# Strided attention and AFNO mixing: the first 64 rows of v by another queue, and a later start of the doubled stores

## The chip, the cores and the metric

The kernel runs on one core of a Trainium2 chip. The metric is device time in microseconds (us) of one execution, here the median of several executions. Lower is better. The profile's own clock starts with the core's first instruction; its span is the time from there to the last instruction.

## The reference

Batch 8, 8 heads, 576 tokens, head dimension 64; then a Fourier mixing layer over the 512 model columns, of which only the first 64 frequencies carry weights. All inputs and the output are fp32.

```
scores = scale * q @ k.T                       # (B, H, S, S)
mask: heads 0-3  0 <= i-j < 32                 # local
      heads 4-7  i >= j and i % 32 == j % 32   # strided
x  = softmax(where(mask, scores, -1e9)) @ v    # to (B, S, 512)
X  = rfft(x, axis=1);  Y = zeros
Y[:, :64] = einsum('bmd,mde->bme', X, w_r + i*w_i)
u  = x + irfft(Y)
out = u + relu(u @ w_ch)                       # fp32
```

The two weight tensors w_r and w_i have 64 x 512 x 512 fp32 values each, 134 MB together: most of what is read.

## The kernel before

All work is put in order by hand (`manual_schedule`): each engine runs its instructions in the order in which the program text emits them, and waits only for semaphores of the data that it needs.

**Loading.** Inputs are read as fp32 and written to SBUF as fp16, the conversion being done by the transfer. All such loads are issued by GpSimd (POOL), one after another: q, k, v of the strided heads (`load_str`, lines 222 to 226), of the local heads (`load_loc`, line 233), and the weights (`w_fetch`, lines 187 to 194). `load_str` puts v, q and k of a batch into slots of the tile `ring`. Each slot holds 72 rows (4 heads x 18 blocks of 32 tokens) of 2048 values. For the first two batches rows 0 to 63 come singly for each batch (line 224, 256 KB of fp16), rows 64 to 71 for both at once (line 226, 64 KB); later batches come in pairs (line 222, 512 KB). SyncE (SP) loads the constants cT (the Fourier table, rows of 1152 bytes) and cMl (a mask), ScalarE's queue (ACT) loads cI (the identity) and the masks cM6 and cM5 (line 109).

**Start.** The order in the text is: `load_str(0, 1)`, ACT's constants, `load_str(1, 1)`, SP's constants, `strided_tokens()` (two small fills and a rearranging copy of cT on POOL, lines 331 to 333), `load_str(2, 2)`, and the first weights. POOL therefore stands at the copy of cT before it issues the loads of batch 2. Meanwhile VectorE (DVE) clears a tile (line 820), TensorE (PE) turns the identity 14 times as filler (line 823), and then `str_front(0)` turns v, q and k of batch 0 on PE, with evacuations by DVE and ACT. `str_v(0, 0)` comes first; it needs all 72 rows of v (PE at line 280).

**Middle.** Strided attention for 8 batches, then local attention, interleaved with products of the spectra with the weights ("modes", lines 601 and 644). Weights live in a ring of buffers, and three early weight pairs lie as guests in tiles that are used later: pair 7 lies in the tile with the tag "YT" (8 KB per partition). POOL issues a weight load when PE has read the buffer's former content.

**Tail.** After the last weight, 18 items are computed in the order of `items`: for each, PE adds the last spectra to two accumulators, ACT (and POOL for one half) makes the ReLU part (`v_done`), and DVE adds the two halves and SP stores them (`u_done`, lines 1094 to 1122). An item is two times 128 rows x 512 columns of fp32, 256 KB each. Items 0 to 9 store each half as soon as it is added, in rows of 2 KB (line 1120). From item 10 to 15, `double(k)` holds: the two items of a pair (even and odd output rows of the same batches) are put side by side in SBUF and are stored together by the second one, as two stores of 512 KB whose rows are 4 KB (line 1109). Items 16 and 17 store both halves at once in rows of 2 KB (line 1122).

Of the kernel before, what the change touches and what calls it, by code (L numbers as in the profile page):

```python
# [10 lines left out]
FP = mybir.dt.float32  # L11
# [45 lines left out]
def kernel(  # L57
# [10 lines left out]
    nc = tc.nc  # L68
# [3 lines left out]
    big = ctx.enter_context(tc.tile_pool(name="big", bufs=1))  # L72
# [63 lines left out]
    ring = pat.tile([128, 12, 2048], F16, name="ring")  # L136
# [73 lines left out]
    def loc_in(b, vi):  # L210
        t = ring[:, ds(2 * (b % 6), 2), :].rearrange("p n x -> p (n x)")
        return t[:, ds(1152 * vi, 1152)]

    def load_str(b, nb):
        for vi in (2, 0, 1):
            n = 3 * (b % 4) + SLOT[vi]
            two = ring[:, n : n + 4 : 3, :]
            src = SRC[vi][b - b % 2 : b - b % 2 + 2, 4:8].rearrange(
                "b h (c r) d -> (h c) b (r d)", r=32
            )  # L220
            if nb == 2:
                nc.gpsimd.dma_start(two[0:64], src[0:64])
            else:
                nc.gpsimd.dma_start(ring[0:64, n, :], src[0:64, b % 2])
            if b % 2 == 0:
                nc.gpsimd.dma_start(two[64:72], src[64:72])
# [27 lines left out]
    def act_copy(out, in_):  # L254
        nc.scalar.activation(out=out, in_=in_, func=ACTF.Copy)  # L255
# [4 lines left out]
    def str_q(b, g):  # L260
        qn, qT = str_in(b, 0), qTs[b % 2]
        tp = psum("tp", half=True)
        for i in range(8):
            nc.tensor.transpose(
                tp[:, ds(72 * i, 72)],
                qn[:, ds(128 * (8 * g + i), 128)],
                idn[0:72, 0:72],
            )
        nc.vector.tensor_copy(
            out=qT.rearrange("p (h r c) -> p r h c", h=4, r=16)[:, ds(8 * g, 8)],  # L270
            in_=tp[:, 0:576].rearrange("p (r h c) -> p r h c", h=4, c=NCB),
        )
# [32 lines left out]
    def str_k(b, j):  # L305
        str_turn(b, 1, j)

    def str_v(b, j):
        str_turn(b, 2, j)

    def str_back(b, part):
        tp = psum("tp", half=True)
        tv = tp.rearrange("p (g x) -> p g x", x=128)
        vg = v16[b % 2]
        js = (1, 2) if part else (0,)
        for i, j in enumerate(js):
            a, z = JG[j]
            for h in range(4):
                nc.tensor.transpose(
                    tv[:, 4 * i + h, :],  # L320
                    vT[:, ds(72 * a + h * (z - a) * NCB, 128)],
                    idn,
                )
        n = 90 if part else 108
        (act_copy if part else nc.vector.tensor_copy)(
            out=vg[0:n, ds(4 * js[0], 4 * len(js)), 2:130],
            in_=tv[0:n, 0 : 4 * len(js), :],
        )
# [461 lines left out]

    psum_pools(tp=3, sc=3, av=2)
    load_str(0, 1)
    const_load(nc.scalar, "cI", "cM6", "cM5")
    load_str(1, 1)
    const_load(nc.sync, "cT", "cMl")
    strided_tokens()
    load_str(2, 2)
    w_fetch()

    def str_front(b):  # L800
        return [
            lambda: str_v(b, 0), lambda: str_v(b, 1),
            lambda: str_v(b, 2), lambda: str_q(b, 0),
            lambda: str_back(b, 0),
            lambda: str_back(b, 1), lambda: str_q(b, 1),
            lambda: str_k(b, 0),
            lambda: str_k(b, 1), lambda: str_k(b, 2),
        ]
# [12 lines left out]
    fill = psum("tp", half=True)  # L821
    for i in range(14):
        nc.tensor.transpose(fill[0:64, ds(64 * i, 64)], idn[0:64, 0:64], idn[0:64, 0:64])
    first = str_front(0)
    for i, w in enumerate(first):
        w()
# [43 lines left out]
    for b in range(B):  # L870
# [12 lines left out]
        n = 0  # L883
        nm = NMODES[b]
        for mi in range(nm):
# [3 lines left out]
            n = upto  # L889
# [120 lines left out]
    for n, i in enumerate([3, 5, 7] + list(range(8, 21))):  # L1010
        b, t = n // 2, n % 2 * 2
# [42 lines left out]
    def out_rows(b, t):  # L1054
        if t < 4:
            steps = [[2 * DM, 128], [(S + 64) * DM, 2], [1, DM]]
            first = 256 * (t // 2) + t % 2
        else:
            steps = [[DM, 128], [2 * S * DM, 2], [1, DM]]
            first = 512  # L1060
        return bass.AP(
            tensor=out.tensor, offset=out.offset + (S * b + first) * DM, ap=steps
        )

    def double(k):
        return 10 <= k < 16

    def both_rows(b, t):
        return bass.AP(
            tensor=out.tensor,  # L1070
            offset=out.offset + (S * b + 64 * (b % 2) + 256 * (t // 2)) * DM,
            ap=[[2 * DM, 128], [1, 2 * DM]],
        )
# [20 lines left out]
    def u_done(k):  # L1094
        bs, t = items[k]
        up, rl = ups.pop(k), rls.pop(k)
        if not osbs:
            osbs.append(pw.tile([128, 2 * NWBUF, 2, DM], FP, tag="w", bufs=1, name="osb"))
        a = k % (2 * NWBUF)
        if double(k):  # L1100
            two = osbs[0][:, a - t % 2 : a - t % 2 + 2].rearrange(
                "p s h d -> p (s h) d"
            )
            for j in range(2):
                nc.vector.tensor_tensor(
                    out=two[:, 2 * j + t % 2], in0=up[:, j], in1=rl[:, j], op=AluOp.add
                )
                if t % 2:
                    nc.sync.dma_start(
                        both_rows(bs[j], t),  # L1110
                        two[:, 2 * j : 2 * j + 2].rearrange("p h d -> p (h d)"),
                    )
            return
        osb = osbs[0][:, a]
        for j in halves:
            nc.vector.tensor_tensor(
                out=osb[:, j], in0=up[:, j], in1=rl[:, j], op=AluOp.add
            )
            if k < 10:
                nc.sync.dma_start(out_rows(bs[0], t)[:, j], osb[:, j])  # L1120
        if k >= 10:
            nc.sync.dma_start(out_rows(bs[0], t), osb)

    flush()
# [23 lines left out]
    for k in range(2):  # L1148
        if k:
            u_early(k)  # L1150
        new_rows(k, ups[k], yys)
        u_done(k)
    for k in range(2, LAST + 2):
        if k == 7:
            held = psum("p", pair=True)[:, 0]
            spec_z(3, 1, held)
            act_copy(zzs[1], held)
        early = 2 if k == 2 else k - 1 if k > 3 else 0
        if k <= LAST:
            v_early(k)  # L1160
        if k > 3:
            u_early(early)
        if k <= LAST:
            new_rows(k, vps[k], zzs)
        if k == 2:
            u_early(k)
        if early:
            new_rows(early, ups[early], yys)
        if k <= LAST:
            v_done(k)  # L1170
        if early:
            u_done(early)
# [31 lines left out]
```

## Time and profile before

| | us |
|---|---|
| device time, median of 3 (range) | 424.64 (424.12 to 424.69) |
| the profiled execution | 424.68 |
| its span | 422.9 |
| PE, DVE, ACT, POOL busy | 327.6, 236.0, 219.8, 111.9 |
| first load of v issued by POOL, L224 | 1.24 to 1.93 |
| first product of the last weight, PE L644 | 390.76 |
| first store issued, SP L1120 | 394.98 |
| last store issued, SP L1122 | 417.7 |

The profile's slices show the share of busy time of each engine and the bytes that the 16 DMA engines wrote per second. For a load that turns fp32 into fp16 the bytes counted are those written, half of those read. The DMA share can exceed 1, since packets of one engine overlap. A "landing" is the time from the issue of a transfer to its completion.

### The profile page before, as it was taken

How to read it: one execution, taken by the hardware profiler on the slowest of the kernel's cores; microseconds unless marked ns; L12 is line 12 of the kernel's file. 1: busy time of each engine (PE TensorE's matmuls, PEld its weight loads, DVE VectorE, ACT ScalarE, POOL GpSimd, SP SyncE). 2: the span in 40 equal slices, each digit the busy share in tenths (PEclk: the TensorE clock that was granted, in tenths of full speed). 3: DMA queues.
4: the chain of work that ended last, by engine and by line, in shares of the span. 5: the costliest groups of instructions: out<-in, count | busy, mean ns of one | idle time of the engine just before them, and what ended most of it. 6: DMA issues, size and time to landing. Idle time of an engine off the chain costs nothing.

```text
span 422.9 us, 9776 instructions
## 1 busy us (share of the span) xinstructions
PE 327.6 (77%) x4156; PEld 202.2 (48%) x4156; DVE 236.0 (56%) x485; ACT 219.8 (52%) x407; POOL 111.9 (26%) x183
## 2 busy tenths in 40 slices
PE   3977878679999298789775858586679839888993
PEld 3865767564666155556533425253335413445320
DVE  3888768950364234555315527656276455555895
ACT  1777768742666166576653413532163345444783
POOL 7432333322421011113121211211112212210583
PEclk9999979956999779899989969999689978999998
DMA  8999999999999999999999999999999999997598
GB/s 148 212 214 213 214 212 213 210 211 211 214 213 213 214 215 214 215 213 215 211 215 214 213 215 213 215 212 213 214 213 215 214 213 215 212 214 155 211 357 326
DMA packets 29674, 91.62 MB, mean 217 GB/s; under 512 B 3968, under 2 KB 4736, under 8 KB 29632
## 3 DMA queue, kind: packets, MB, share of 16 engines
q0 software_dynamic: 24624, 81.28, 96.8%
q1 hardware_dynamic: 4576, 9.65, 6.1%
q8 instruction: 32, 0.52, 0.5%
q10 hardware_dynamic: 432, 0.08, 0.1%
q14 instruction: 10, 0.08, 0.0%
HBM read 162.83 MB, written 9.44 MB: 407 GB/s over the span
## 4 chain that ended last, share of the span: by engine, by line
DMA 56%; PE 27%; DVE 8%; issue 4%; ACT 3%; POOL 1%; DVEq 0%; POOLq 0%; ACTq 0%
DMA wring<-in_moe_w_i_dram 42%; DMA ring<-in_q_dram 7%; PE y L601 7%; DMA wring<-in_moe_w_r_dram 4%; PE sc L743 3%; PE p L1030 2%; DMA ring<-in_k_dram 2%; PE p L1050 2%; PE tp L417 2%; PE sc L463 1%; PE sc L536 1%; DVE xb L245 1%; DVE yy L778 1%; DMA ring<-in_v_dram 1%; PE sc L479 1%
## 5 line engine op out<-in xcount | busy, mean ns | idle before, releaser
L601 PE MATMUL y<-wring,X 128*32 128x512 f16 (+1 forms) x424 | 47.9, 443 | 34.8 <-DMA wring<-in_moe_w_i_dram 34.7
L190 POOL DMA_DIRECT2D wring<-in_moe_w_r_dram x39 | 23.6, 604 | 188.3 <-PE y L601 163.2
L255 ACT ACTIVATE yr<-y 128x512 f16<-128x512 f32 x28 | 16.7, 597 | 57.3 <-PE y L601 55.6
L601 PEld LDWEIGHTS <-X 128*32 128x32 f16 (+1 forms) x448 | 21.9, 143 | 47.9 <-DMA wring<-in_moe_w_i_dram 34.4
L753 DVE COPY xo<-tp 128x512 f16<-128x512 f16 x32 | 22.1, 692 | 36.2 <-PE tp L751 36.2
L743 PE MATMUL sc<-w_cp,xT 128*128 128x512 f16 x128 | 37.1, 413 | 1.5 <-DVE xT L711 1.4
L245 DVE TENSOR_TENSOR xb<-av,rec 90x256 f16<-90x256 f32 (+2 forms) x80 | 36.0, 450 | 2.8
L752 ACT ACTIVATE v<-sc 128x512 f16<-128x512 f32 x32 | 19.1, 597 | 35.4 <-PE sc L743 35.4
L493 ACT ACTIVATE PL<-sc 128x480 f16<-128x480 f32 (+1 forms) x48 | 26.9, 578 | 17.2 <-PE sc L479 16.7
L244 DVE RECIPROCAL rec<-av 90x4 f32<-90x4 f32 (+2 forms) x80 | 14.6, 183 | 34.7 <-PE av L508 24.3
L424 DVE COPY qT<-tp 128x576 f16<-128x576 f16 x16 | 11.9, 752 | 36.7 <-PE tp L417 36.7
L1004 DVE TENSOR_TENSOR xo<-p,xo 128x1024 f16<-128x1024 f32 x16 | 19.6, 1225 | 20.3 <-PE p L786 20.3
L190 POOL DMA_DIRECT2D wring<-in_moe_w_i_dram x42 | 25.4, 606 | 9.7 <-DMA wring<-in_moe_w_i_dram 5.8
L382 ACT ACTIVATE PL<-sc 90x360 f16<-90x360 f32 (+1 forms) x48 | 22.7, 490 | 6.6 <-PE sc L375 6.2
L255 ACT ACTIVATE v<-p 128x1024 f16<-128x1024 f32 x16 | 16.4, 1023 | 18.3 <-PE p L786 18.3
L417 PE MATMUL tp<-cI_s,ring 64*64 64x64 f16 x864 | 23.5, 201 | 2.3 <-DVE qT L424 1.7
L255 ACT ACTIVATE v<-tp 128x640 f16<-128x640 f16 (+1 forms) x24 | 19.0, 807 | 10.5 <-PE tp L451 7.9
L463 PE MATMUL sc<-cMl_s,cI_s 128*128 128x480 f16 (+1 forms) x48 | 19.3, 401 | 4.7 <-ACT PL L493 3.1
L417 PEld LDWEIGHTS <-ring 64*64 64x64 f16 x864 | 18.7, 115 | 8.5 <-issue 4.4
L255 ACT ACTIVATE kz<-tp 64x360 f16<-64x360 f16 (+1 forms) x32 | 18.9, 592 | 6.2 <-PE tp L417 5.2
L1090 POOL TENSOR_TENSOR rl<-rl,xo 128x512 f32<-128x512 f32 x15 | 17.1, 1157 | 15.5 <-DVE rl L1083 13.0
L536 PEld LDWEIGHTS <-xb 108*128 108x128 f16 (+2 forms) x176 | 15.7, 107 | 11.2 <-DVE xb L245 6.2
(153 smaller groups left out, 763.6 us busy)
## 6 DMA issues: line engine op xcount, KB each, us to landing
wring<-in_moe_w_r_dram POOLq DMA_DIRECT2D x17, 1024.0 KB, 18.1
wring<-in_moe_w_i_dram POOLq DMA_DIRECT2D x16, 1024.0 KB, 22.4
wring<-in_moe_w_i_dram POOLq DMA_DIRECT2D x24, 512.0 KB, 17.6
wring<-in_moe_w_r_dram POOLq DMA_DIRECT2D x22, 512.0 KB, 15.2
out_dram<-osb SPq DMA_DIRECT2D x20, 256.0 KB, 2.3
out_dram<-osb SPq DMA_DIRECT2D x8, 512.0 KB, 3.5
ring<-in_v_dram POOLq DMA_DIRECT2D x8, 288.0 KB, 13.2
ring<-in_q_dram POOLq DMA_DIRECT2D x8, 288.0 KB, 13.5
```

The source lines that it names most:

```text
L190: nc.gpsimd.dma_start(dst, rows)
L245: nc.vector.tensor_tensor(out=dst, in0=val.rearrange("p h (q c) -> p h c q", c=4), in1=rec[0:n, 0:pieces] .to_broadcast((n, pieces, 64)) . ...
L255: nc.scalar.activation(out=out, in_=in_, func=ACTF.Copy)
L382: nc.scalar.activation(out=PS[0:n, ds(POFF[t], 4 * n)], in_=scp[0:n, 0 : 4 * n], func=ACTF.Exp, scale=SCALE,)
L417: nc.tensor.transpose(tp[ds(64 * hp, 64), ds(64 * i, 64)], qn[ds(64 * hp, 64), ds(64 * (9 * g + i), 64)], idn[ds(64 * hp, 64), ds(64 * hp, ...
L463: nc.tensor.matmul(scp[:, 0 : n * times].rearrange("p (h x) -> p h x", h=times), idn, mask_rows("cMl", n, times), start=True, stop=False,)
L493: nc.scalar.activation(out=dst, in_=src, func=ACTF.Exp, scale=SCALE)
L536: nc.tensor.matmul(xp[:, ds(192 * cp, 192)].rearrange("p (f m) -> p f m", f=3), xb[b][0:n, base + t, ds(128 * cp, 128)], F[0:n, :, t, :], ...
L601: nc.tensor.matmul(yp[ds(a, 32), :], Xh[half][pr, c].rearrange("p b r (h m) -> p (b r h) m", h=2)[:, :, mm % 32], wt[pr, XC[c], :], start= ...
L743: nc.tensor.matmul(vp, xT[:, ch], w_chs["cp"][:, ch, :], start=(ch == 0), stop=(ch == 3),)
L753: nc.vector.tensor_copy(out=xo.rearrange("p (h q c) -> p h q c", h=2, c=4), in_=tp[:, 0:512].rearrange("p (h c q) -> p h q c", h=2, c=4),)
L1004: nc.vector.tensor_tensor(out=xo, in0=up[:, 0:n], in1=xo, op=AluOp.add)
```

## The change

In `load_str`, the load of rows 0 to 63 of v of batch 0 is no longer issued by POOL with conversion, but by SP without: into a new fp32 tile with the tag "YT", 64 rows of 8 KB. As `load_str(0, 1)` stands ahead of SP's constants, it is SP's first transfer. Before `str_front(0)`, DVE copies columns 0 to 1023 of it to `ring` as fp16 and ACT columns 1024 to 2047. Rows 64 to 71 come as before. In the tail, `double` holds from item 12 on, so items 10 and 11 store each half by itself like the items before them: four stores of 256 KB in place of two of 512 KB.

```diff
@@ load_str
+    firsts = []
     def load_str(b, nb):
         for vi in (2, 0, 1):
...
             if nb == 2:
                 nc.gpsimd.dma_start(two[0:64], src[0:64])
+            elif b == 0 and vi == 2:
+                v_first = big.tile([128, 2048], FP, tag="YT", name="v_first")
+                nc.sync.dma_start(v_first[0:64], src[0:64, 0])
+                firsts.append((ring[0:64, n, :], v_first[0:64]))
             else:
                 nc.gpsimd.dma_start(ring[0:64, n, :], src[0:64, b % 2])
@@ before str_front(0)
         nc.tensor.transpose(fill[0:64, ds(64 * i, 64)], idn[0:64, 0:64], idn[0:64, 0:64])
+    to, frm = firsts[0]
+    nc.vector.tensor_copy(out=to[:, 0:1024], in_=frm[:, 0:1024])
+    act_copy(to[:, 1024:2048], frm[:, 1024:2048])
     first = str_front(0)
@@ tail
     def double(k):
-        return 10 <= k < 16
+        return 12 <= k < 16
...
-            if k < 10:
+            if k < 12:
                 nc.sync.dma_start(out_rows(bs[0], t)[:, j], osb[:, j])
-        if k >= 10:
+        if k >= 12:
             nc.sync.dma_start(out_rows(bs[0], t), osb)
```

## The prediction

> **What bounds the kernel now.** I read the page's slices first, then the DMA table, then windows of a quarter of a microsecond at both ends, then the timelines there.
>
> ```profile
> DMA  8999999999999999999999999999999999997598
> GB/s 148 212 214 213 214 212 213 210 211 211 214 213 213 214 215 214 215 213 215 211 215 214 213 215 213 215 212 213 214 213 215 214 213 215 212 214 155 211 357 326
> q0 software_dynamic: 24624, 81.28, 96.8%
> q1 hardware_dynamic: 4576, 9.65, 6.1%
> ```
>
> No engine is full (PE 77%), but the DMA engines are, and at a flat 213 GB/s from the second slice to the 36th. POOL's queue alone has 81.28 MB: 81.28 MB / 213 GB/s = 381.6 us. So up to the last weight, DMA sets the time. POOL's waits for PE (163 us at L190) are waits for free buffers behind a queue that never empties. The shortest landing of a weight load in the middle is this, in the window 100 to 108:
>
> ```profile
> DMA to landing us min/median/max: 8.1/10.0/11.8
> ```
>
> A microsecond saved at the start reaches the last weight as long as some microseconds of loads stand in that queue; here they do. Now the start:
>
> ```profile
> 0.75 0.33 SPq L109 DMA_DIRECT2D cT_s<-cT  x1
> ...
> 1.24 0.69 POOL L224 DMA_DIRECT2D ring<-in_v_dram  x1 [0.79 <-POOLq L1188]
> ...
> 6.99 0.98 PEld L280 LDWEIGHTS <-ring 72*128 72x128 f16 x16 [2.95 <-DMA ring<-in_v_dram]
> ...
> 7.28 1.17 POOL L333 COPY PL<-cT_s 128x576 f16<-128x576 f16 x1
> ```
> ```profile
> 1.50:3.90 2.40, 0.68 (x13) 0.68 (x14) 0.65 (x1) 1.28 (x1) 2.40 (x5) 1.00 0.85 141
> 4.00:8.00 4.00, 1.16 (x20) 1.02 (x17) 0.42 (x1) 0.12 (x1) 3.11 (x8) 1.00 1.02 174
> ```
> ```profile
> 3.50:3.75 0.25, 0.25 (x9) 0.25 (x8) 0.00 (x0) 0.00 (x0) 0.25 (x2) 1.00 0.00 0
> 3.75:4.00 0.25, 0.25 (x8) 0.25 (x6) 0.00 (x0) 0.00 (x0) 0.25 (x1) 1.00 0.17 34
> 4.00:4.25 0.25, 0.18 (x4) 0.04 (x1) 0.00 (x0) 0.00 (x0) 0.25 (x2) 1.00 1.11 222
> ```
>
> The last two numbers of a window are the DMA share and GB/s. Only constants move from 1.5 to 3.4; then the DMA engines stand still until POOL's first load comes at 3.9, about 2.0 us after its issue ended. From 4 to 8 they do 174 instead of 213 GB/s: (213-174) x 4 = 156 KB, 0.73 us lost. Then the tail:
>
> ```profile
> 409.75:410.00 0.25, 0.25 (x5) 0.05 (x2) 0.25 (x1) 0.25 (x2) 0.25 (x1) 1.00 0.61 221
> 410.00:410.25 0.25, 0.25 (x4) 0.13 (x3) 0.25 (x2) 0.25 (x1) 0.25 (x1) 1.00 0.00 0
> 410.25:410.50 0.25, 0.25 (x3) 0.03 (x1) 0.25 (x2) 0.25 (x2) 0.25 (x1) 1.00 0.00 0
> 410.50:410.75 0.25, 0.25 (x6) 0.05 (x4) 0.25 (x1) 0.25 (x1) 0.25 (x2) 1.00 1.06 426
> ```
> ```profile
> 407.89 0.33 SPq L1120 DMA_DIRECT2D out_dram<-osb  x1
> 409.68 3.32 SPq L1109 DMA_DIRECT2D out_dram<-osb  x4
> ```
>
> From 396 to 421 the stores fill the DMA engines too, except for a short dip at 404 and a hole of 0.6 us at 409.9: item 10 stores nothing and waits for item 11. From 410.5 on they never rest until 421.1.
>
> **The first load: what leaves POOL's queue.** 256 KB of fp16 at 213 GB/s is 1.23 us of the stream that sets the end. POOL's issue of it (0.69 us) goes as well, so each later load of the start is issued some 0.6 us earlier. That can fill the dip at 5.25 to 5.75 (69 and 117 GB/s, (144+96) x 0.25 = 60 KB, 0.28 us) at least; all of the lost 0.73 us at best. I take 0.28.
>
> **What it costs instead.** 512 KB of fp32 on SP. No row shows such a load. Nearest below: the stores from 405 to 409, 2 KB rows of plain fp32 at 383 to 387 GB/s, 1.36 us. Nearest above: loads into 64 partitions that write 213 GB/s, 2.46 us. I take the former, a plain copy like this one. It can use the time before 3.9. From 1.5 to 3.9, 2.4 us x 141 GB/s = 338 KB of constants move, 0.88 us at 385 GB/s: 1.5 us free by bytes, and then nothing spills over. By the DMA share, 0.85 of a full 1.06, only 0.45 us is free, and 0.9 us spills into the stream. I take half, 0.45 us. Sum for the start: -1.23 + 0.45 - 0.28 = **-1.06 us**. Ends: -1.23 - 0.73 = -1.96, and -1.23 + (2.46 - 0.45) = +0.78.
>
> The Trainium skill speaks against my price: "SBUF — State Buffer", section Door 1, says that partitions 0 to 63 reach only 8 of 16 DMA ports, some 218 GB/s written. The trace's 213 GB/s agrees in number. By this rule the load takes the upper price, and it is the first rival below. Yet the local heads' loads, to 128 partitions, also go at 210 (96 to 104), so the rows don't show which end limits.
>
> **What is hidden.** The two copies, of 1024 values in 64 partitions: nearest rows are ACT's 128x1024 copy from PSUM (1.02 us), DVE's 1024-wide add at L1004 (1.23) and its memset of 1171 words (1.03). Between 0.5 and 1.3 us, I take 1.1 for both side by side. If SP's load lands 2.7 to 3.8 us after 0.75 (the 512 KB store lands in 2.7), the copies end by 4.6 to 5.7. Rows 64 to 71, now POOL's first load, land about 5.5 (5.0 after issue before, minus the 256 KB ahead of them), so PE starts at about 5.7 instead of 6.99. Nothing is added for that and nothing subtracted: PE waits for q and for weights again and again. Were PE a microsecond late instead, the queue's 8.1 us would cover it. Behind the copies on DVE and ACT stand only evacuations of that same v. On SP, cT and cMl are moved behind the new load, and POOL waits for cT at L333. Before, cT landed at 3.05 and POOL came at 7.28, now at about 6. Behind L333 are batch 2's loads. The eight loads ahead of them (5 x 256 + 3 x 64 KB) last 7.1 us, from 4.35 to 11.4; allowing 1.17 for the copy, 0.59 for the issue and 2.0 to the first byte, cT may land as late as 7.6 for nothing. The guest pair 7 waits for the copies, done long before.
>
> **Does the end follow?** After the last weights the whole tail moves along. From 386 to 391 PE is busy 1.64 + 1.78 + 0.41 of 5 us: it idles 1.17 us, so it can follow 1.06 us, barely.
>
> **The tail.** Before: the stores restart at 410.50; six of 512 KB at 406 GB/s (411 to 417) take 1.29 us each, the last two, in 2 KB rows, 1.39 at 378: 410.50 + 7.74 + 2.77 = 421.01, as seen. After: item 9's bytes end at 409.90; the four new stores are issued from 408.5 on, in time, at 383 GB/s 0.684 us each, until 412.64. The first pair is then items 12 and 13, whose first store is issued at 412.07 (as DVE's first add of item 13 ends at 412.05); 0.82 us from issue to bytes, as at 409.68, gives 412.89. A hole of 0.25 us is left. 412.89 + 4 x 1.29 + 2.77 = 420.82: **-0.19 us**. Ends: no hole at all, -0.44; the hole as wide as before and the 2 KB rows' price (2.74 against 2.58) on top, +0.16. The two more issues (0.33 us each) lie in SP's idle time.
>
> **Sum.** -1.06 - 0.19 = -1.25 us. Against the profiled 424.68 (span 422.9 and 1.8 around it) that is 423.4; this execution lies 0.04 above the median, so I leave it at that.
>
> **Rivals.**
> 1. The load writes only 213 GB/s. Then 2.46 - 1.5 = 0.96 us spills, the start gains 0.27 and the dip is not filled: with the tail -0.46, **424.2**. For it: the flat 213 of every 64-partition load. Against: loads to 128 partitions do the same, and stores do 385.
> 2. The other side: the constants and the new load choke each other in front of POOL's stream. Small rows hold DMA engines by time and not by bytes (share 0.85 at 141 GB/s), so 2.46 - 0.45 = 2.0 us spills; start +0.78, tail -0.19: **425.3**. It decides once more than 1.23 us spills, and grows one for one where cT lands past its limit. For it: cM5 with 22.5 KB landed 5.4 us after its issue, cM6 with 27 KB in 2.4. Against: DMA stands still from 3.5 to 3.9.
> 3. The change doesn't do what it says, because the last modes are bound by PE: PE has little idle time from 378 to 387. Then only the tail counts: **424.5**. Against: PE waits for the last two weights, 0.58 and 0.59 us.
>
> **How the numbers follow.** Forecast 0.60, rival 1 0.20, rival 2 0.13, rival 3 0.07. Time 423.4; the forecast's own range, from its unknown prices, is 422.6 to 424.2. The range for 8 in 10 reaches to rival 2: 422.6 to 425.2. About 0.2% (0.85 us) is what a measurement of this kernel can tell from no change, so faster means under 423.79: most of the forecast and a little of rival 1, 0.60. Slower means over 425.49: rival 2 with a late cT, 0.12. The rest, 0.28, is the same.
>
> **What would show it.** The new load landing at 3.5 to 4.6; the first 213 GB/s quarter earlier than about 8; PE at L280 by 5.7; cT landed before POOL's copy; the last weight's first product at 389.7 instead of 390.76; the hole at 410 gone and a smaller one at 412.7; the last store landing some 1.2 us earlier. Wrong if SP's load lands after 5, if GB/s stays low up to 8 as before, if POOL waits at L333 for cT, or if PE at L644 no longer waits for DMA near the end.

## The result, and the profile after

| | us |
|---|---|
| device time after, median of 11 (range) | 425.80 (425.42 to 426.36) |
| before beside it, median of 11 (range) | 424.69 (424.12 to 425.52) |
| ratio after / before, 95% interval | 1.0023, 1.0014 to 1.0032 |
| profiled execution after, its span | 425.64, 423.8 |
| the same before | 424.68, 422.9 |

The kernel became slower, by 1.1 us. The forecast was 423.4, and 425.8 lies outside its range too. The page's slices and queue, after:

```profile
GB/s 170 201 211 212 214 212 213 209 213 210 213 215 210 215 216 211 216 213 214 212 214 214 213 215 213 215 211 208 214 213 215 214 213 214 213 214 164 199 370 323
q0 software_dynamic: 24544, 81.01, 96.7%
```

The flat stream of some 213 GB/s is as before, and so is its length but for 0.27 MB. The first slice moves more (148 before) and the second less (212 before). Now the start of the kernel after, in its timeline (start and duration in us, engine, line, operation, and in brackets the idle time before it and what ended that):

```profile
0.75 0.58 SPq L227 DMA_DIRECT2D v_first<-in_v_dram  x1
1.36 0.76 POOL L232 DMA_DIRECT2D ring<-in_v_dram  x1 [0.90 <-POOLq L1197]
1.39 0.56 SPq L109 DMA_DIRECT2D cT_s<-cT  x1
...
5.55 1.06 ACT L261 ACTIVATE ring<-v_first 64x1024 f16<-64x1024 f32 x1 [2.16 <-DMA v_first<-in_v_dram]
5.55 0.73 DVE L831 CAST ring<-v_first 64x1024 f16<-64x1024 f32 x1 [3.40 <-DMA v_first<-in_v_dram]
...
6.40 1.24 POOL L339 COPY PL<-cT_s 128x576 f16<-128x576 f16 x1
...
7.50 1.12 PE L286 MATMUL tp<-cI_s,ring 72*128 72x72 f16 x16 [3.84 <-DMA ring<-in_v_dram]
```

The new load's data is there at 5.55, 4.8 us after its issue where 2.7 to 3.8 were forecast, and after 5, which was to show that the prediction is wrong; the copies follow at once and end at 6.6, but PE starts only at 7.50 (7.02 before): it waits for POOL's first load, rows 64 to 71, issued at 1.36 and landed at 7.36. Now the DMA issues and queues of the first 20 us (size and time to landing; for a queue its packets, MB and share of 16 engines), after:

```profile
q0 software_dynamic: 968, 2.86, 81.3%
q1 hardware_dynamic: 368, 0.74, 15.8%
...
v_first<-in_v_dram SPq DMA_DIRECT2D x1, 512.0 KB, 4.8
cT_s<-cT SPq DMA_DIRECT2D x1, 144.0 KB, 5.0
cMl_s<-cMl SPq DMA_DIRECT2D x1, 64.0 KB, 6.5
```

And before:

```profile
q0 software_dynamic: 1081, 3.25, 87.2%
q1 hardware_dynamic: 288, 0.21, 4.3%
...
cT_s<-cT SPq DMA_DIRECT2D x1, 144.0 KB, 2.3
cMl_s<-cMl SPq DMA_DIRECT2D x1, 64.0 KB, 2.2
```

POOL's queue (q0) lost 0.26 MB of work, yet has moved 0.39 MB less by 20 us: it is behind by 0.13 MB, 0.6 us at 213 GB/s, where it was to be ahead. The constants that landed 2.2 us after their issue now take 5.0 and 6.5. Wider stretches tell when the stream fell behind. The columns are the stretch, its length, the busy time of PE, PEld, DVE, ACT and POOL, the clock, the DMA share and GB/s. Before, then after:

```profile
0.50:8.00 7.50, 1.93 (x30) 1.79 (x30) 1.50 (x2) 1.41 (x2) 5.87 (x12) 1.00 0.82 139
8.00:20.00 12.00, 10.50 (x151) 9.26 (x149) 9.92 (x28) 7.38 (x15) 6.11 (x11) 1.00 1.06 210
20.00:30.00 10.00, 8.13 (x146) 6.78 (x146) 8.67 (x25) 8.12 (x19) 3.66 (x7) 1.00 1.06 213
```

```profile
0.50:8.00 7.50, 1.46 (x23) 1.35 (x24) 1.81 (x2) 2.34 (x2) 6.63 (x12) 1.00 0.87 172
8.00:20.00 12.00, 10.65 (x147) 9.56 (x145) 9.64 (x25) 6.63 (x13) 5.39 (x10) 1.00 1.13 201
20.00:30.00 10.00, 8.28 (x152) 6.80 (x148) 8.70 (x25) 8.17 (x19) 3.46 (x6) 1.00 1.07 207
```

The load adds 524 KB and takes away 262 KB: 262 KB more must be moved. By 8 us (172 - 139) x 7.5 = 247 KB more are moved, nearly all of it. Then, long after the load has landed, the same stream of POOL loads runs slower at a higher share: 9 x 12 + 6 x 10 = 168 KB are lost. (262 - 247 + 168) KB / 213 GB/s = 0.86 us. POOL's weight loads around 100 us arrive 0.90 us later than the same loads before (by the packets of its queue, counted back from the last one). So two things went wrong, and the second is not in the prediction at all. At the end of the stream, in the chain of waits of the kernel after:

```profile
382.32 9.59 DMA wring<-in_moe_w_i_dram
...
392.05 0.41 PE y L650 x8
```

Before, this load began to hold up the chain at 381.04 and PE multiplied from 390.76 on: 1.29 us earlier. Read off the quarter windows, the stores' last bytes come 30.15 us after that product (at 422.2), 30.33 before (421.09), so the tail gained 0.2 us. In the quarter windows after:

```profile
413.75:414.00 0.25, 0.25 (x2) 0.10 (x2) 0.25 (x2) 0.25 (x1) 0.25 (x1) 1.00 0.81 303
414.00:414.25 0.25, 0.25 (x3) 0.00 (x0) 0.25 (x1) 0.25 (x2) 0.25 (x1) 1.00 0.30 115
414.25:414.50 0.25, 0.25 (x4) 0.10 (x2) 0.25 (x2) 0.25 (x1) 0.25 (x2) 1.00 0.94 377
```

Only this dip of some 0.25 us is left of the hole of 0.6 us that was at 409.9.

### The profile page after: what moved, and what is told of

It is laid out like the page before. It is cut to its first block, busy times and chain, and to the rows that moved or that the text cites. A ratio compares the mean times of both kernels' runs of the same rounds, so it can differ in the third digit from the quotient of the medians.

```text
span 423.8 us, 9786 instructions
## 1 busy us (share of the span) xinstructions
PE 328.9 (78%) x4156; PEld 202.8 (48%) x4156; DVE 236.9 (56%) x486; ACT 220.9 (52%) x408; POOL 111.9 (26%) x182
## 4 chain that ended last, share of the span: by engine, by line
DMA 58%; PE 23%; DVE 9%; issue 4%; ACT 2%; POOL 1%; DVEq 0%; POOLq 0%
DMA wring<-in_moe_w_i_dram 49%; PE y L607 6%; DMA ring<-in_q_dram 5%; DMA wring<-in_moe_w_r_dram 4%; DVE xb L251 2%; DVE kz L293 2%; PE p L1039 2%; PE sc L749 2%; PE sc L542 2%; PE p L1059 2%; POOL wring L190 1%; DVE rec L250 1%; ACT X L261 1%; PE sc L469 1%; PE tp L423 1%
## 5 line engine op out<-in xcount | busy, mean ns | idle before, releaser
L607 PE MATMUL y<-wring,X 128*32 128x512 f16 (+1 forms) x424 | 49.1, 453 | 34.4 <-DMA wring<-in_moe_w_i_dram 34.3
L749 PE MATMUL sc<-w_cp,xT 128*128 128x512 f16 x128 | 38.2, 424 | 1.4 <-DVE xT L717 1.4
L430 DVE COPY qT<-tp 128x576 f16<-128x576 f16 x16 | 11.9, 752 | 36.0 <-PE tp L423 36.0
L1096 ACT ACTIVATE rl<-p 128x512 f32<-128x512 f32 x35 | 18.9, 595 | 3.4 <-PE p L1059 1.8
```

Source lines behind the costliest of these rows:

```text
L607: nc.tensor.matmul(yp[ds(a, 32), :], Xh[half][pr, c].rearrange("p b r (h m) -> p (b r h) m", h=2)[:, :, mm % 32], wt[pr, XC[c], :], start= ...
L749: nc.tensor.matmul(vp, xT[:, ch], w_chs["cp"][:, ch, :], start=(ch == 0), stop=(ch == 3),)
```

## The experiments

Every run was timed beside runs of the kernel before on the same chip; "+" is the difference of the medians. Diffs of start runs are against the first part alone.

**1. The two parts, each alone.** start_only is the kernel after with `10 <= k < 16`; tail_only is the kernel before with `12 <= k < 16`.

> The start's half of the change alone (doubled stores from item 10 on, as before). Theory S, the start costs what the whole change costs and the tail gives a little back: 0.2 to 0.4 us above the changed kernel, that is 1.2 to 1.5 us above the kernel before, first product of the last weight near 392.0. Rival, the tail is what costs: equal to before, first product of the last weight near 390.8.

> The tail's half alone (POOL loads all of v as before). Theory S: 0.2 to 0.4 us below the kernel before, the hole at 410 replaced by a smaller one some 2.7 us later. Rival, the tail costs: 0.9 to 1.2 us above before.

Start alone: 426.17 against 424.81, +1.36, ratio 1.0031 [1.0020, 1.0043]. Tail alone: 424.56, -0.25, ratio 0.9997 [0.9988, 1.0006]. Together +1.1, the whole change. The tail's gain lies within the interval of no change, but its windows show what was worked out:

```profile
410.00:410.25 0.25, 0.25 (x3) 0.10 (x1) 0.25 (x2) 0.25 (x2) 0.25 (x1) 1.00 1.05 401
...
412.50:412.75 0.25, 0.25 (x3) 0.00 (x0) 0.25 (x1) 0.25 (x2) 0.25 (x1) 1.00 0.28 107
```

The hole at 410 is filled, and a smaller one came at 412.6, where the prediction had 412.64 to 412.89. In the packet records the last store ends 30.25 us after the last weight's first product in tail_only and 30.27 in after, but 30.45 in before and 30.44 in start_only: 0.2 us gained both times.

**2. Without the load, and with both loads.** The price of the new load is measured from both sides: taken out altogether (no_first, which computes with zeros in these rows), and put on top of POOL's load (extra).

```diff
# no_first
-                nc.sync.dma_start(v_first[0:64], src[0:64, 0])
+                nc.vector.memset(ring[0:64, n, :], 0.0)
# extra
+                nc.gpsimd.dma_start(ring[0:64, n, :], src[0:64, b % 2])
```

> The load of rows 0 to 63 of v of batch 0 is left out altogether and the rows are cleared by DVE; the tail as before. It prices what leaves POOL's queue. Theories P and C both: 1.2 to 1.9 us below the kernel before (1.23 us of bytes and at most the 0.73 us lost from 4 to 8). Rival N, the removal is worth little because the end of POOL's stream doesn't follow its bytes: within 0.4 us of before.

> POOL's load of the same rows is kept, and SP's is added in front of SP's constants; the rest as in the start's half alone. It prices the SP load by itself. Theory E: the sum of leaving out (0.85 us below before) and the start's half (1.36 above), 2.0 to 2.3 us above before. Rival I, much of the load fits into the idle time before 3.9 us: less than 1.4 us above before.

no_first: 423.93 against 424.81, ratio 0.9980 [0.9972, 0.9989], -0.88. extra: 426.90 against 424.97, 1.0041 [1.0029, 1.0053], +1.93. In the stream, taking 256 KB out of POOL's queue is worth what was predicted: it is 1.30 us earlier at 100 us (1.23 predicted) and 1.20 at 380; in its profiled execution the first product of the last weight comes 0.67 us earlier than before (390.09 against 390.76). The time fell by less than the 1.2 to 1.9 us expected. The load itself costs 1.36 + 0.88 = 2.24 us, or 1.93 on top of before: more than its whole predicted price of 1.36.

**3. More partitions, and the place in the queue.** wide puts the same 512 KB into all 128 partitions, which mixes up the rows of v; late and wide_late put the load behind SP's constants; halves splits it over SP's and ACT's queues, each to half of the partitions; two_4k makes two loads of it. A load in pieces of 2 KB (rows2k) has no result.

```diff
# wide
+                flat = bass.AP(tensor=v.tensor, offset=v.offset + 4*S*D, ap=[[1024, 128], [1, 1024]])
+                nc.sync.dma_start(v_first[:, 0:1024], flat)
# late
     const_load(nc.sync, "cT", "cMl")
+    nc.sync.dma_start(firsts[0][1], firsts[0][2])
# halves
+                nc.sync.dma_start(v_first[0:64, 0:1024], src[0:64, 0, 0:1024])
+                nc.scalar.dma_start(v_first[64:128, 0:1024], src[0:64, 0, 1024:2048])
# two_4k
+                for i in range(2):
+                    cols = ds(1024 * i, 1024)
+                    nc.sync.dma_start(v_first[0:64, cols], src[0:64, 0, cols])
```

> The start's half, but SP's 512 KB go to 128 partitions in rows of 4 KB instead of 64 partitions in rows of 8 KB; the rows of v of batch 0 are mixed up by it. Same bytes, same queue, same place. Theory P, the load is slow because 64 partitions take only some 213 GB/s of fp32: it lands 0.8 to 1.1 us earlier than 4.8 us after its issue, and the time is 0.8 to 1.1 us below the start's half alone. Theory C, whatever the shape, the load pushes the constants with their small rows into POOL's stream, and these cost by time and not by bytes: within 0.3 us of the start's half alone.

> The start's half alone with SP's order turned: cT and cMl first, then the load of v. Theory E, the load costs the DMA engines' time that its packets hold (2.1 us each), wherever it stands: within 0.4 us of the start's half alone, 0.9 to 1.7 us above before, though cT lands at about 3.1 again. Theory C, the constants that it pushes into POOL's stream are what costs: at least 0.6 us below the start's half alone.

> The start's half alone, but columns 0 to 1023 of the rows go by SP to partitions 0 to 63, and columns 1024 to 2047 by ACT's queue (ahead of its constants) to partitions 64 to 127; the copies bring both halves together. If transfers of two queues to the two halves of the partitions run side by side: as the wide load, 0 to 0.6 us above before. If they come one after the other: as the start's half alone, 1.0 to 1.6 us above before. A sum over both (bytes alone) would be 0.4 us above, as the wide load.

> The start's half alone, with SP's load cut into two loads of 1024 columns each, both to partitions 0 to 63: pieces of 4 KB, as in the wide load, but 64 partitions, as in the change. Theory P (partitions): together the packets hold each DMA engine about 2.1 us, and the time stays 1.0 to 1.6 us above before. Rival K (pieces of 8 KB are slow): about 1.35 us, and the time is at most 0.6 us above before, as with the wide load.

> The wide load (128 partitions, rows of v mixed up) behind SP's constants. If the two prices add up, the 0.8 us that 64 partitions cost and the 0.5 us that the pushed-back constants cost, it is 0.2 us below to 0.2 us above the kernel before: the load then costs what it takes out of POOL's queue. If the late place helped only because a narrow load leaves gaps that constants fill: as the wide load, 0.3 to 0.6 us above before. If the load found free time: 0.5 us or more below before.

| run | median, before | ratio, 95% interval | + us |
|---|---|---|---|
| wide | 425.30, 424.81 | 1.0007 [0.9999, 1.0016] | 0.5 |
| late | 425.67, 424.97 | 1.0016 [1.0006, 1.0025] | 0.70 |
| halves | 426.39, 424.97 | 1.0032 [1.0020, 1.0043] | 1.42 |
| two_4k | 425.71, 424.96 | 1.0020 [1.0009, 1.0031] | 0.75 |
| wide_late | 425.76, 424.96 | 1.0022 [1.0008, 1.0035] | 0.80 |

Both the partitions and the place seem to matter, but they don't add up: wide_late was expected at -0.2 to +0.2 (part 5 shows where its 0.8 us is lost). late is 0.50 us below start_only, between its two theories. In halves the two loads and the constants land one after the other, and ACT's constants, too, stand behind a half there (cI landed 2.4 us after its issue before):

```profile
v_first<-in_v_dram SPq DMA_DIRECT2D x1, 256.0 KB, 3.7
v_first<-in_v_dram ACTq DMA_DIRECT2D x1, 256.0 KB, 5.1
cT_s<-cT SPq DMA_DIRECT2D x1, 144.0 KB, 5.4
...
cI_s<-cI ACTq DMA_DIRECT2D x1, 32.0 KB, 6.2
```

two_4k was to tell piece size from partitions and couldn't: it lay between the two. So the cost was made larger.

**4. Five dead loads of each form** in the kernel before, behind SP's constants, which nothing reads (`five` is a new tile ahead of `wring`).

```diff
+    for i in range(5):
+        at = v.offset + (8 * i + 4) * S * D
# narrow: 64 partitions, 8 KB
+        ap=[[2048, 64], [1, 2048]]
# wide: 128 partitions, 4 KB
+        ap=[[1024, 128], [1, 1024]]
# pieces: 64 partitions, 4 KB
+        ap=[[2048, 64], [1024, 2], [1, 1024]]
```

> The kernel before, with five more loads of 512 KB of fp32 on SP behind its constants, each to 64 partitions in rows of 8 KB, into memory that is not yet used; nothing reads them. The price of one load, five times over. If it is the 2.0 us that the start's half minus the left-out load shows: 9 to 12 us above before. If a narrow load in the midst of POOL's stream costs its bytes alone (1.3 us): 6 to 7.5.

> The same five loads to 128 partitions in rows of 4 KB. Both theories: 1.3 us each, 6 to 7.5 us above before. Under theory P the five narrow loads are 3 to 5 us dearer than these; if place and not shape made the difference, the two are within 1 us.

> The same five loads to 64 partitions, each row of 8 KB cut into two pieces of 4 KB by its places in SBUF. Theory P (partitions): as the five narrow loads, within 1 us. Rival K (pieces of 8 KB): as the five wide loads, within 1 us.

Against 424.83: narrow 436.16, ratio 1.0268 [1.0253, 1.0283], 2.27 us for each load; wide 433.26, 1.0192 [1.0177, 1.0207], 1.69 each; pieces 436.44, 1.0270 [1.0252, 1.0287], 2.32 each. 64 partitions against 128 is worth 0.6 us for 512 KB, and the size of the pieces nothing that shows. POOL's stream at 100 us agrees: 11.4, 8.4 and 11.9 us late. Even wide's 1.69 is above the 1.3 that was expected of its bytes. The windows from 8 to 12 of narrow and of wide, at the same DMA share:

```profile
8.00:12.00 4.00, 1.12 (x16) 0.97 (x16) 1.05 (x7) 0.83 (x2) 2.33 (x5) 1.00 1.07 207
```

```profile
8.00:12.00 4.00, 1.12 (x16) 0.98 (x16) 1.58 (x7) 0.83 (x2) 2.07 (x5) 1.00 1.07 243
```

**5. Where is the rest lost?** The byte balance of the first section agrees with the shift of POOL's stream at 100 us, and shows two groups (KB against before; "behind" is (more to move - moved by 8 us + lost from 8 to 30 us) / 213 GB/s; the windows are rounded to 1 GB/s, some 0.05 us; the last two columns are the shift of POOL's packets, counted back from the last one):

| run | more to move | more moved by 8 us | lost 8 to 30 us | behind, us | later at 100 us by | later at 380 us by |
|---|---|---|---|---|---|---|
| start_only | 262 | 240 | 136 | 0.74 | 0.74 | 0.80 |
| halves | 262 | 210 | 226 | 1.31 | 1.38 | 1.47 |
| extra | 524 | 285 | 300 | 2.53 | 2.66 | 2.65 |
| late | 262 | 202 | 8 | 0.32 | 0.29 | 0.72 |
| two_4k | 262 | 232 | 36 | 0.31 | 0.29 | 0.25 |
| wide | 262 | 352 | 90 | 0.00 | 0.00 | 0.84 |
| wide_late | 262 | 255 | -4 | 0.01 | 0.00 | 0.68 |
| no_first | -262 | 8 | -12 | -1.32 | -1.30 | -1.20 |

At 100 us wide and wide_late have lost nothing against before; the 0.74 us of start_only are gone. What makes wide_late dear comes later: wide, late and wide_late lose 0.4 to 0.8 us between 100 and 380 us, most of it from 280 to 320.

The loss from 8 to 30 us is a spell in which POOL's packets themselves last longer. From the trace's DMA records, the mean ns of one 4 KB packet of POOL's queue by the time of its start (us):

```
              8-10 10-12 12-14 14-16 16-18 18-20 20-22 22-24 24-26 26-28
before         334   324   324   324   324   326   324   324   324   326
start_only     344   346   331   362   347   382   333   334   334   324
late           328   323   324   330   329   332   328   328   326   324
two_4k         324   326   359   331   327   327   324   324   324   324
```

324 ns is the even beat of the stream in these runs outside such spells; wide, too, has a spell (330 to 358 ns from 12 to 24 us). What starts the spell was asked of three more runs: the load first and in 4 KB pieces (to 64 partitions, one transfer); the load first but dead, with POOL's load kept and no copies; and the load between cT and cMl.

```diff
# first_pieces
+                rows = bass.AP(tensor=v.tensor, offset=..., ap=[[2048, 64], [1024, 2], [1, 1024]])
# first_dead
-                firsts.append((ring[0:64, n, :], v_first[0:64]))
+                nc.gpsimd.dma_start(ring[0:64, n, :], src[0:64, b % 2])
# mid
+    const_load(nc.sync, "cT")
+    nc.sync.dma_start(firsts[0][1], firsts[0][2])
+    const_load(nc.sync, "cMl")
```

> As the first part alone, but the same 512 KB go to the same 64 partitions in one transfer of 128 pieces of 4 KB instead of 64 of 8 KB. In the traces so far POOL's 4 KB packets last 324 ns each from 10 us on in before, but 331 to 382 ns from 8 to 26 us in the first part alone, 136 KB or 0.64 us lost; with two loads of 4 KB rows (two_4k) and with the load behind the constants (late) they mostly last 324. Theory S1, the 8 KB pieces leave the DMA engines in disorder: no such spell here, 210 GB/s from 8 to 20 us, +0.75 us as two_4k. Theory S2, it is one big load ahead of everything: the spell is there, 202 GB/s from 8 to 20, +1.3 to +1.4 us. Theory N, chance of an execution: the profile says nothing of the times, and times lie at about +1.0 for all.

> Before, plus SP's 512 KB load in front, which nothing reads: POOL's load stays, no copies on VectorE and ScalarE, and the product waits for nothing new. Against extra (+1.93 us, 195 GB/s from 8 to 20 us), which has the copies too. If the spell of long packets comes from the load: 195 to 202 GB/s from 8 to 20 us and +1.8 to +2.0 us. If it comes from the copies, or from the later work on PE behind them: 210 GB/s and +1.2 to +1.4 us.

> As the first part alone, with SP's load between cT and cMl instead of in front of both. If the place ahead of all other bytes makes the spell, none here: 210 GB/s from 8 to 20 us and +0.7 us, as with the load behind both (late). If the pushed-back constants make the cost, cMl alone (64 KB of 208) is pushed back: between the two, near late, +0.7 to +0.9 us. If any 8 KB load near the start does it: 202 GB/s and +1.3 us.

Against 424.79: first_pieces 426.52, ratio 1.0041 [1.0028, 1.0054], +1.73; first_dead 427.32, 1.0067 [1.0052, 1.0081], +2.53, more than either of its theories had; mid 425.67, 1.0019 [1.0010, 1.0028], +0.88. Their windows from 8 to 20 us, in this order:

```profile
8.00:20.00 12.00, 10.47 (x129) 9.33 (x127) 8.94 (x24) 5.96 (x12) 5.67 (x10) 1.00 1.12 199
```

```profile
8.00:20.00 12.00, 9.94 (x126) 8.93 (x127) 8.30 (x22) 5.65 (x12) 7.06 (x14) 1.00 1.12 195
```

```profile
8.00:20.00 12.00, 10.46 (x124) 9.33 (x125) 9.03 (x23) 6.55 (x13) 5.17 (x9) 1.00 1.08 211
```

The spell is there with 4 KB pieces, so the 8 KB pieces don't make it. It is there without the copies and with nothing waiting for the load, so neither the copies nor PE make it. It is gone when one constant load of 144 KB goes ahead on SP: mid loses 8 KB from 8 to 30 us, first_pieces 222 and first_dead 290. So the spell goes with the load's place ahead of SP's constants; of the runs with the load there, two_4k hardly shows it (36 KB) and wide less than the others (90 KB). It is not all of the cost: mid's stream is only 0.11 us late at 100 us, but 0.62 at 380. No version with a load on SP is faster than before. By the sum of the two, mid with the shorter tail would come to about +0.7; this was not run.

## Why the prediction was wrong

- **What bounds the kernel: right.** The shift of POOL's stream reaches the last weight, though not to the tenth: in start_only 0.74 us at 100 us, 0.80 at 380 and 0.62 at the last weight's first product, in no_first 1.30, 1.20 and 0.67. two_4k lost another 1.1 us at its last five loads. "Does the end follow?": PE does; after, it still waits for both last weights.
- **-1.23 for the 256 KB: right.** no_first moved the stream by 1.30 us at 100 us, though the time by 0.88 only.
- **-0.28 for the dip: wrong.** By its windows no_first had only 8 KB more by 8 us and 12 KB by 30, some 0.1 us.
- **+0.45 for the load: this step failed.** "I take half": a price of 1.36, of which 0.9 was to lie in free time. start_only against no_first shows 2.04 us in the stream at 100 us (0.74 + 1.30) and 2.24 in the medians of the time. By the byte balance no_first stood 262 + 8 = 270 KB ahead at 8 us and start_only 262 - 240 = 22 KB behind: 292 KB or 1.37 us. The other 0.67 us is the spell from 8 to 30, for which the sum has no term. So even without the spell the spill is three times the one taken. The price was mis-sized, and not the free time: at the 2.27 us measured in part 4, a spill of 1.37 leaves 0.9 us in free time, just what was taken. wide gives nearly the same: 1.69 less 270 - 90 = 180 KB or 0.85 us. Both are estimates, for they take the price in a full stream as the price at the start. With them the term is 2.27 - 0.9 + 0.67 = 2.04. In after the load's 64 packets run from 2.11 to 4.59, 2.48 us, and the constants land 2.7 and 4.3 us later than before.
- **The price of an unseen transfer** was taken from the row of the same type (plain fp32 stores, 383 GB/s), where the row of the same partitions was nearer. Five in a full stream cost 2.27 us each to 64 partitions and 1.69 to 128. **Rival 1's cause is shown**, worth 0.6 us; at the kernel's start, where other loads compete, wide against start_only shows 0.74 in the stream at 100 us. Its time, 424.2, was still too low: it took 1.5 us as free and had no spell. "SBUF — State Buffer" of the Trainium skill, section Door 1, says that partitions 0 to 63 reach 8 of 16 DMA ports, some 218 GB/s; an estimate by that page is 524 KB / 218 GB/s = 2.40 us. The 2.27 measured is near it, and wide's lower price agrees.
- **Rival 2 named the sign and nearly the number** (425.3): 2.0 us of spill, as in the stream here. Its cause, constants and load in each other's way, is borne out only in part, and its number is luck: 2.46 - 0.45 comes out like 2.27 - 0.9 + 0.67. The constants do land late. But with cT ahead of the load (mid) or both ahead (late) the bytes moved by 8 us are only 30 KB more and 38 KB fewer than in start_only, while the loss from 8 to 30 falls from 136 to 8 KB in both. What the order saves is the spell, which no rival had. "cT late past its limit" didn't happen: it landed at 6.3, as POOL came to it.
- **"DMA stands still from 3.5 to 3.9" was misread.** In the packet records of before, the first 16 packets of POOL's queue start between 2.97 and 3.37 and last 0.74 to 1.19 us. A window counts a packet where it starts, hence its 0.00 from 3.50 to 3.75; with each packet spread over its duration, the share there is 1.00.
- **The tail: right.** -0.19 against 0.2 in the windows and -0.25 in the medians of tail_only, too little to be told from nothing by time alone. With it, rival 3's 424.5 is what the tail does alone (424.56).
- **What was hidden: right in its cost, wrong in its times.** The copies took 1.06 and 0.73 us side by side and hold up nothing. PE came 0.5 us later and not 1.3 earlier, since POOL's first load landed 6.0 us after its issue. That this delay costs nothing in the end isn't shown by a run of its own; first_dead, where PE waits for no copy, is no faster.

Open is why the packets last longer in such a spell; the records show that they do, not where an engine waits. Shorter ones also come later, around 284 to 310 us, in the profiled executions of after, wide, late, wide_late and mid, and hardly in that of start_only. In after one adds 0.3 to 0.4 us to the shift at the end (0.90 at 100 us, 1.27 at 380). As after and start_only run the same program up to the tail, they go at least in part with the execution. But the medians of wide, late, wide_late and mid (+0.5 to +0.88) lie near their profiled executions, so there the later loss is hardly rare; what brings it stays open. With one profile for each kernel, two_4k's missing spell may be chance as well.

## What to carry to other kernels

A load on another queue takes its time out of the stream all the same (1.69 to 2.32 us each for the five dead ones), so price it as if it stood in the full stream, unless the trace shows the engines idle; before calling them idle, look at how long the packets last that started just before. Here the row with the same partitions priced the unseen transfer better than the row of the same type (2.46 and 1.36 us, 2.27 measured); where a price of a microsecond must be known, put five of them in and divide. Make a byte balance by stretches, (more to move - more moved) / the stream's rate: it tells in which stretch a shift of the end arises, here much of it long after the load had landed. Follow the stream to its end, for some versions lost as much on the way as others at the start.

## What the runs showed that was not expected

- A load ahead of all other bytes lengthened another queue's packets for 18 us after it, from 324 ns to as much as 382 in a stretch of 2 us (start_only), with the DMA share up from 1.06 to 1.12 and 136 to 300 KB lost, less only in wide and two_4k. With one 144 KB load ahead of it (mid) 8 KB were lost.
- With SP's load issued at 0.75, POOL's queue began later as well: in first_dead POOL's first load is issued at 1.25, as before, and yet the queue's first packet starts at 4.97 (2.97 before), and the DMA engines moved only 121 GB/s from 4.0 to 4.5, where before they moved 215.
- Two queues to two halves of the partitions gained nothing (halves, +1.42 against +1.36), with ACT's constants behind a half as well.
